# One planned order for all engines, turns of x on TensorE, and an early load of half of u, in a kernel of convolution and attention

## Chip, cores and metric

One core of a Trainium2 chip. The metric is the device time of one execution in microseconds, the median of several; a profile of one execution gives the views quoted here. The runs below were in the fast state, but for one of replan (591.53 us) and three of the kernel before beside the experiments (699.75, 693.45 and 691.0 us); ratios use fast runs alone. They are the mean time of one kernel's fast runs over the mean of the kernel before in the same rounds on the same chip, so they are not quite the ratio of the medians quoted beside them.

## The reference

Two independent halves share the input length of 2048. The left half of the output is a long convolution whose kernel K is generated from six parameter arrays, the right half is attention over eight keys at stride two.

```python
def conv(u, A, B, C, log_dt, Dskip):            # u: 1 x 2048 x 1024, A, B, C complex 1024 x 128
    dt = exp(log_dt)[:, None]
    P = exp((dt * A)[:, :, None] * arange(2048))
    K = einsum("dn,dnl,dn->dl", C, P, dt * B).real
    y = irfft(rfft(u_padded) * rfft(K_padded))[:2048]
    return y + u * Dskip
def attention(x, wqkv, wo):                     # x: 1 x 2048 x 1024, 32 heads of 32
    q, k, v = (x @ wqkv) ...                    # each query sees keys at offsets 0, 2, ..., 14 back
    return softmax(q . k / sqrt(32)) @ v  ... @ wo
return concatenate([conv(...), attention(...)], axis=-1)      # bf16
```

## The kernel before

It has two stages. In stage 1, QKV and the generation of K are written in one hand-made interleaving. In stage 2 two generators, convolution and attention, are advanced in turn by step counts.

```python
# stage 1: x comes by sixteen DMA transposes; V is 2048 matmuls of 32 output rows
def load_x(self, par):
    for kt in range(8):
        nc.sync.dma_start_transpose(out=self.xT[:, kt, par*1024:(par+1)*1024], in_=self.xv[par][:, kt*128:(kt+1)*128])
# ... V, in v():
for kt in range(8):
    for h in range(4):
        nc.tensor.matmul(ps[32*h:32*h+32, ...], lhsT=self.xT[:, kt, t0:t0+32], rhs=self.wv[:, kt, :, h, :], ..., tile_position=(0, 32*h))

# stage 2, convolution: an FFT in steps; what step 1 makes of u and K goes out to HBM and comes back
def step1(self, hf, name, src):
    ...
    nc.tensor.matmul(pz[:, i, :], lhsT=self.l1[:, mt, :], rhs=src[:, ..., :], ...)   # 512 columns
    self.bal.copy(zs[...], pz[:], 1024)
    nc.sync.dma_start(out=Z[:, n2:n2+4, :], in_=zs[64*b:64*b+64])
def middle(self, hf):
    # load(p): zu, zk from HBM, issued by GpSimd; forward(p-1); back(p-2)
    for x in range(2):
        V.tensor_tensor(out=pr[:, x], in0=F[1][:], in1=kf[:, x:x+1, :].to_broadcast(...), op=ALU.mult)  # F[1] in PSUM
    ...
# stage 2, attention: one S and one O bank
for ct in range(8):
    S = self.pp.tile([128, 512], F32, name="S")
    for b in range(-1, NB):                      # 9 key blocks x 4 heads: 36 matmuls of 32 rows, 8 to 40 columns
        for h in range(4):
            nc.tensor.matmul(S[hs, o:o+n], lhsT=ks[hs, ct, kb:kb+32], rhs=qs[hs, ct, qa:qa+n], ..., tile_position=(32*h, 32*h))
    ...                                          # Exp (ACT), mask (DVE), two matmuls with ones, 36 for the values, Ln and Exp (ACT), product (DVE)
    yield
...
drive(conv(), 64 + 36 + 16, at.gen(), 80)        # advances the two generators by counts
```

The softmax here doesn't subtract the row's maximum and nothing guards it: scores larger than these inputs give would overflow.

## Time and profile before

| | before |
|---|---|
| time, median (range) | 691.88 us (686.53 to 692.02), 3 runs; with the runs beside the changed kernel 690.08, 4 runs |
| profiled span | 688.6 us |
| busy: PE, DVE, ACT, POOL | 485, 376, 369, 105 us |
| DMA | 116.19 MB |
| mean granted clock of TensorE | 0.846 |

The prediction below reads the page of this profile. Two windows split the span at the end of kernel generation and at the first work on K; the columns are busy us of PE, its weight loads, DVE, ACT and POOL with instruction counts, the granted clock, DMA share and GB/s.

```profile
0.00:242.70 242.70, 185.96 (x3706) 104.37 (x3707) 183.36 (x314) 186.51 (x297) 29.36 (x35) 0.95 0.40 100
...
271.00:688.60 417.60, 276.76 (x5646) 125.65 (x5645) 192.44 (x281) 176.14 (x301) 76.03 (x128) 0.77 0.80 210
```

The late window is where time lies idle: 418 us for 277 us of PE work at a clock of 0.77, with DMA at 0.80.

### The profile page before, as it was taken

How to read it: one execution, taken by the hardware profiler on the slowest of the kernel's cores; microseconds unless marked ns; L12 is line 12 of the kernel's file. 1: busy time of each engine (PE TensorE's matmuls, PEld its weight loads, DVE VectorE, ACT ScalarE, POOL GpSimd, SP SyncE). 2: the span in 40 equal slices, each digit the busy share in tenths (PEclk: the TensorE clock that was granted, in tenths of full speed). 3: DMA queues.
4: the chain of work that ended last, by engine and by line, in shares of the span. 5: the costliest groups of instructions: out<-in, count | busy, mean ns of one | idle time of the engine just before them, and what ended most of it. 6: DMA issues, size and time to landing. Idle time of an engine off the chain costs nothing.

```text
span 688.6 us, 23065 instructions
## 1 busy us (share of the span) xinstructions
PE 484.9 (70%) x10268; PEld 247.5 (36%) x10268; DVE 376.1 (55%) x595; ACT 369.0 (54%) x608; POOL 105.4 (15%) x163
## 2 busy tenths in 40 slices
PE   0284989899999785303775962569788885779866
PEld 0031546556556455102343431224332341223432
DVE  4758878768777802221544431245855862576442
ACT  3585798698798623102554432334646752656441
POOL 5400111010110000000010020000545644350000
PEclk9997999999999898655885955687997997699979
DMA  9980322132231164999585699375997899894685
GB/s 145 258 165 16 93 79 92 59 102 72 79 103 66 54 223 136 255 181 253 136 272 177 199 224 178 91 231 145 328 270 199 243 218 253 220 264 99 185 223 161
DMA packets 103891, 116.19 MB, mean 169 GB/s; under 512 B 46992, under 2 KB 84112, under 8 KB 102128
## 3 DMA queue, kind: packets, MB, share of 16 engines
q1 hardware_dynamic: 95376, 88.63, 49.3%
q0 software_dynamic: 8416, 26.10, 13.9%
q8 instruction: 80, 1.31, 0.8%
q14 instruction: 19, 0.16, 0.1%
HBM read 58.59 MB, written 50.33 MB: 158 GB/s over the span
## 4 chain that ended last, share of the span: by engine, by line
PE 35%; DVE 15%; DMA 15%; ACT 14%; issue 10%; SPq 3%; POOL 0%; ACTq 0%; DVEq 0%
PE cp L579 6%; PE ps L383 6%; DMA Zv<-vs 4%; PE psv L399 4%; DMA big<-Zv 4%; PE cp L627 3%; DVE OR L195 3%; PE O L566 3%; PE S L550 2%; PE pk L239 2%; PE cp L653 2%; DVE OL L224 2%; PE cp L669 2%; DVE OL L223 2%; DMA Kd<-K 2%
## 5 line engine op out<-in xcount | busy, mean ns | idle before, releaser
L383 PE MATMUL ps<-xT,w 128*128 128x512 bf16 x512 | 129.7, 403 | 53.7 <-DMA xT<-in_B_x_dram 32.8
L659 DVE TENSOR_TENSOR pr<-cp,kf 128x1024 bf16<-128x1024 f32 x64 | 75.7, 1219 | 42.7 <-ACT kf L499 33.5
L383 PEld LDWEIGHTS <-w 128*128 128x128 bf16 x512 | 49.1, 102 | 119.1 <-issue 61.9
L550 PE MATMUL S<-qs,ks 32*32 32x40 bf16 (+2 forms) x2304 | 38.9, 185 | 60.3 <-ACT pe L553 20.9
L579 PE MATMUL cp<-wosb,oT 128*128 128x512 bf16 x256 | 62.4, 397 | 4.7 <-ACT zs L499 2.8
L570 ACT ACTIVATE ln<-O 128x256 f32<-128x256 f32 x64 | 24.6, 384 | 73.2 <-PE O L566 66.3
L643 POOL DMA_DIRECT2D zk<-Zk x64 | 38.2, 600 | 164.3 <-PE S L550 82.9
L399 PE MATMUL psv<-wv,xT 128*32 128x256 bf16 x2048 | 62.2, 273 | 0.0
L550 PEld LDWEIGHTS <-ks 32*32 32x32 bf16 x2304 | 27.5, 96 | 93.7 <-issue 72.9
L643 POOL DMA_DIRECT2D zu<-Zu x64 | 38.1, 600 | 138.9 <-PE S L550 117.3
L572 DVE TENSOR_TENSOR oT<-O,ln 128x256 bf16<-128x256 f32 x64 | 27.0, 422 | 54.4 <-ACT ln L571 54.4
L627 PE MATMUL cp<-big,l 128*128 128x512 bf16 x128 | 43.2, 450 | 18.2 <-DMA big<-in_A_u_dram 12.9
L399 PEld LDWEIGHTS <-xT 128*32 128x32 bf16 x2048 | 52.5, 97 | 7.2 <-issue 6.4
L499 ACT CAST vs<-cp 128x1024 bf16<-128x1024 f32 x32 | 32.4, 1012 | 39.8 <-DMA Zv<-vs 26.3
L502 DVE CAST zs<-cp 128x1024 bf16<-128x1024 f32 x36 | 43.0, 1218 | 17.5 <-PE cp L627 17.4
L553 ACT ACTIVATE pe<-S 128x320 bf16<-128x320 f32 x64 | 27.7, 433 | 43.3 <-PE S L550 42.3
L554 DVE TENSOR_TENSOR pm<-pe,mk 128x320 bf16<-128x320 bf16 x64 | 20.3, 320 | 50.8 <-ACT pe L553 32.4
L669 PE MATMUL cp<-pr,m 64*128 64x512 bf16 x256 | 41.2, 423 | 7.7 <-ACT vs L499 5.5
L499 ACT CAST zs<-cp 128x1024 bf16<-128x1024 f32 x28 | 28.0, 1009 | 34.2 <-PE cp L627 22.1
L182 DVE TENSOR_SCALAR PA<-PH 128x1024 int32<-128x1024 int32 (+1 forms) x36 | 27.9, 775 | 27.2 <-ACT TL L186 19.4
L579 PEld LDWEIGHTS <-oT 128*128 128x128 bf16 x256 | 25.2, 102 | 37.2 <-issue 11.8
L653 PE MATMUL cp<-zu,m 128*64 128x512 bf16 x128 | 24.0, 437 | 20.0 <-ACT vs L499 13.2
(105 smaller groups left out, 750.2 us busy)
## 6 DMA issues: line engine op xcount, KB each, us to landing
Zu<-zs SPq DMA_DIRECT2D x32, 256.0 KB, 5.1
Zk<-zs SPq DMA_DIRECT2D x32, 256.0 KB, 5.5
zu<-Zu POOLq DMA_DIRECT2D x64, 128.0 KB, 6.3
zk<-Zk POOLq DMA_DIRECT2D x64, 128.0 KB, 6.1
Zv<-vs SPq DMA_DIRECT2D x64, 128.0 KB, 3.9
big<-Zv SPq DMA_DIRECT2D x16, 512.0 KB, 7.6
w<-in_B_wqkv_dram POOLq DMA_DIRECT2D x16, 256.0 KB, 4.9
QT<-sg SPq DMA_DIRECT2D x16, 256.0 KB, 2.1
```

The lines of the kernel that those rows point to most:

```text
L182: V.tensor_scalar(out=PA[:, 0:n, :], in0=PH[:, 0:n, :], scalar1=16384.0, scalar2=None, op0=ALU.add)
L383: nc.tensor.matmul(ps[:, h, :], lhsT=self.w[ct][:, kt, t, :], rhs=self.xT[:, kt, t0:t0 + 512], start=(kt == 0), stop=(kt == 7))
L399: nc.tensor.matmul(ps[32 * h:32 * h + 32, b * 256:b * 256 + 256].rearrange("p (c d) -> p c d", d=32), lhsT=self.xT[:, kt, t0:t0 + 32], rhs ...
L499: self.nc.scalar.copy(out=out, in_=in_)
L502: self.nc.vector.tensor_copy(out=out, in_=in_)
L550: nc.tensor.matmul(S[hs, o:o + n], lhsT=ks[hs, ct, kb:kb + 32], rhs=qs[hs, ct, qa:qa + n], start=True, stop=True, tile_position=(32 * h, 3 ...
L579: nc.tensor.matmul(po[:, h, :], lhsT=oT[:, ct, tt * 128:(tt + 1) * 128], rhs=self.wo[:, ct, h * 512:(h + 1) * 512], start=(ct == 0), stop= ...
L627: nc.tensor.matmul(pz[:, i, :], lhsT=self.l1[:, mt, :], rhs=src[:, rq * 4 + rp * 2 + i, :], start=True, stop=True)
L643: nc.gpsimd.dma_start(out=t[64 * ri:64 * ri + 64], in_=self.Z[n][hf][4 * p + ri:4 * p + 4:2].rearrange("ab n d -> n ab d"))
L653: nc.tensor.matmul(f[64 * ab:64 * ab + 64, ri, :], lhsT=w[:, ab, 64 * ri:64 * ri + 64], rhs=z[:, ab, :], start=True, stop=True, tile_posit ...
L659: V.tensor_tensor(out=pr[:, x], in0=F[1][:], in1=kf[:, x:x + 1, :].to_broadcast([128, 2, 512]), op=ALU.mult)
L669: nc.tensor.matmul(v[:, ab, :], lhsT=w[rs, t, :], rhs=pr[rs, x, y, :], start=(i == 0), stop=(i == 3), tile_position=(64 * ab, 0), skip_gro ...
```

## The change

The intent is to fill that window. Everything becomes one list of 1813 tasks with dependencies and rings of buffers, and one fixed order for all engines, worked out ahead and stored in the kernel. Within it, x and the parameters are loaded in rows and turned by TensorE; V uses full-width matmuls; what step 1 makes of u and K stays on chip; and half of u is rewritten and loaded into the space that the sine phases leave, while QKV still runs. The core of the diff (cut; the order table and nearly all else left out):

```diff
+ORDER = (
+    "XAAJABEAAABRAUgPaQEhABgOUAA5AFkBgQEcAGQBUQ9YD2QASAFxAdAA5ABsABEC3ACxASkA+QEdAmUPMABBACUCMAJ8AaEPLQI4..."   # cut: 1813 codes
+)
 ...
-    def load_x(self, par):
-        for kt in range(8):
-            self.tc.nc.sync.dma_start_transpose(out=self.xT[:, kt, ...], in_=self.xv[par][:, kt * 128:(kt + 1) * 128])
+    def turn(self, pool, idn, load, put, eng, strided, prio):
+        def mm(e):
+            st["ps"] = ps = self.ps.tile([128, 2, 8, 128], BF, name="ps")
+            for i in range(2):
+                for kt in range(8):
+                    nc.tensor.transpose(ps[:, i, kt, :], st["xn"][:, i, kt * 128:(kt + 1) * 128], idn[:])
 ...
-                for b in range(2):
-                    n2 = 16 * (2 * mt + b) + rq * 4
-                    nc.sync.dma_start(out=Z[:, n2:n2 + 4, :], in_=zs[64 * b:64 * b + 64])
+                def evac(e, pi=pi, w=w):
+                    copy(nc, e, z["t"][:, :, 16 * pi:16 * pi + 16], w["pz"][:].rearrange("x p (g k) -> x k (p g)", g=4))
 ...
+        def load_u(hf, after):
+            src = {}; slot = P(None, 0, ..., [opened if hf else phases, after], take=("big", "b2") if hf else "bu", prio=2.4 + 3 * hf)
 ...
-    drive(conv(), 64 + 36 + 16, at.gen(), 80)
+        seq = plan.order()
+        for t in seq:
+            st["ring"] = t.ring
+            ...
+            t.fn(t.pick)
```

## The prediction

> **What bounds the kernel now.** I read the engine sums first, then the 40 slices, then busy time by stage, the waits, and a stretch of the timeline.
>
> ```profile
> PE 484.9 (70%) x10268; PEld 247.5 (36%) x10268; DVE 376.1 (55%) x595; ACT 369.0 (54%) x608; POOL 105.4 (15%) x163
> ...
> PE   0284989899999785303775962569788885779866
> ...
> DVE  4758878768777802221544431245855862576442
> ...
> PEclk9997999999999898655885955687997997699979
> DMA  9980322132231164999585699375997899894685
> ...
> DMA packets 103891, 116.19 MB, mean 169 GB/s; under 512 B 46992, under 2 KB 84112, under 8 KB 102128
> ```
>
> No engine is full over the span. There are two regimes in it. In the first third (QKV, kernel generation) PE and DVE, and ACT with them, are mostly at 7 to 9 tenths and DMA at 1 to 3. Then comes a hole, and after it everything is at 3 to 7 tenths while DMA is at 7 to 9. Busy time by stage (columns: PE, weight loads, DVE, ACT, POOL, granted clock, DMA share, GB/s):
>
> ```profile
> 62.00:145.00 83.00, 73.76 (x1472) 41.94 (x1471) 68.47 (x119) 68.32 (x123) 5.42 (x6) 0.93 0.24 77
> ...
> 258.00:345.00 87.00, 36.40 (x1176) 22.78 (x1166) 26.05 (x61) 20.77 (x41) 0.00 (x0) 0.69 0.80 193
> 345.00:487.00 142.00, 95.07 (x2402) 47.45 (x2401) 58.05 (x91) 56.12 (x112) 7.80 (x14) 0.71 0.71 190
> 487.00:640.00 153.00, 121.18 (x1857) 47.91 (x1857) 89.97 (x103) 85.61 (x123) 68.22 (x115) 0.87 0.87 232
> ```
>
> The 229 us from 258 to 487 are the soft part: DVE does 84 us of work, ACT 77, PE 131, the last at a clock of 0.7. The waits say why (engine, line, what it waited for: total us, times, longest):
>
> ```profile
> POOL zu L643 <- PE S L550: 117.3, 2, 117.1
> ...
> ACT ln L570 <- PE O L566: 66.3, 50, 7.7
> ...
> DVE oT L572 <- ACT ln L571: 54.4, 41, 6.4
> ...
> PE ps L383 <- DMA xT<-in_B_x_dram: 32.8, 8, 27.0
> ...
> DVE K L299 <- PE pk L239: 28.0, 1, 28.0
> ```
>
> Attention with one S and one O bank goes round PE, ACT, DVE once per tile with little beside it; the spread of K goes through HBM; x arrives by DMA transposes until about 45 us. A stretch of the timeline shows one more:
>
> ```profile
> 412.79 0.39 PE L550 MATMUL S<-qs,ks 32*32 32x40 bf16 x26
> ...
> 418.57 0.18 PE L550 MATMUL S<-qs,ks 32*32 32x32 bf16 x1 [5.40 <-issue]
> ```
>
> PE stops in the middle of a score tile for 5.4 us with nothing to wait for. Such "issue" steps are 9.8% of the chain that ended last (0.098 x 689 = 67 us). My reading, not shown by the view, is that PE's instructions are late: the page has an instruction queue of 80 packets, 1.31 MB, which shares the DMA engines.
>
> **What the Trainium skill says.** (1) "VectorE: DVE Perf Modes", the perf-mode tier table: a tensor_tensor runs two elements a cycle in bf16 from SBUF and one with any PSUM operand. The trace agrees: the product from PSUM (line 659, 1024 elements) takes 1219 ns, the bf16 outer product from SBUF (line 215, 1024 elements) 686. (2) The same page, the three transpose paths: a 128x128 bf16 block takes 390 ns on TensorE and 1309 by DMA. Single transposes aren't in this trace; it shows the sixteen DMA transposes of x being issued over 24 us. (3) "TensorE: Matmul & The Clock Gate", what's actually happening: the array runs at half clock until it has been busy for a window of about 3.4 us, and falls back after an idle one. Agrees: clock 1.00 where PE was 99% busy (145 to 195 us), 0.69 where it was 42% busy. (4) "DMA: Bandwidth & Descriptors", specifications: transfers want 512 B or more for full rate. No view here tests it alone; 46,992 of 103,891 packets are smaller.
>
> **The change part by part.** It rewrites nearly everything into 1813 tasks in one fixed order, so I count work per engine with durations from the rows of before.
>
> PE, warm. Eight 512-column matmuls take 1.83 us (chain rows): Q and K 64 x 1.83 = 117; V, now 256 full-width matmuls instead of 2048 narrow ones, 32 x 1.83 = 59 (before 32 x 1.76: no gain). New: 11 turns of 16 transposes, estimated at 1 us each from 2048 columns at the matmul rate, 11. Kernel products 2048 small matmuls, about 32 with their gaps. Attention 64 x (0.28 + 0.48, start to start near 644 us) = 49. Projection 16 x 3.47 = 56. First FFT step 65,536 columns at 0.215 us per 512, 28. Middle forward: sixteen 256-column matmuls on four tiles instead of four 512-column ones on two, the same 0.46 us, 64 times, 29. Back 32 x 0.9 = 29, last 16 x 0.9 = 14, shift 3. Sum 427.
>
> ACT. Sines 77 (before 80; the trivial phase row is gone), amplitudes 40, Q and K evictions 32, kernel evictions 7, parameters 12, attention 28 + 25 + 27 = 79, table loads about 17. In the order table, 135 of the 221 movable copies carry ACT and 86 DVE: 135 x 1.01 = 136. Sum 400.
>
> DVE. Kernel generation by its rows 164, parameters 26, nine turns 13, six V copies 7, K spread 16, attention 47, other copies 71 x 1.22 = 86, and the middle products 64 x 0.69 = 44 in place of 75.7, because u's spectrum is copied to bf16 first. That copy is 32 new ones on ACT or DVE, so the pair of engines gains nothing from it: 32 us saved for some 36 added. Sum 403.
>
> So ACT + DVE rise from 745 to 803; PE's sum falls from 485 only by being warm. The gain is in packing. What leaves is DMA: Zu and Zk (8.4 MB each, written and read back, 33.5 MB) stay in SBUF, K goes SBUF to SBUF, attention's q and k loads become long runs, and 76 us of POOL issue work (128 loads of Z, 600 ns each, that wait behind PE) go. What comes is the rewriting of u, 4.2 MB in 32,768 pieces of 128 B, placed where DMA was at 0.25. Adding all transfers up I get 85 MB in place of 116.
>
> Phase A, until the kernel is generated. By the order, everything on DVE up to the last kernel product comes first: 164 + 26 + 13 + 7 = 210 us. ACT has 176 there; PE 32 V tasks, 49 halves of Q and K tiles, turns and kernel products, 59 + 90 + 11 + 32 = 192. So DVE bounds it, if only just. It ran at 78 to 82% in this stage before; with phases triple buffered, two ER buffers and the order made for it I take 93%, 226 us, and 7 us before its first useful work (before: 7.05). End at about 233. Before, DVE finished the same work near 242, and the first K copy came at 271 because the kernel matmuls sat late in PE's queue. Here seven Q and K tiles are held back instead, interleaved with step one of u, so PE has something to do while K is spread.
>
> Phase B, the rest. PE 427 - 192 = 235, ACT 400 - 176 = 224, DVE 403 - 210 = 193. PE leads by little. Three engines at this load, in fixed queues, over three large PSUM tiles and the S and O banks (which scores and values may now trade for a large one): I take 89% for PE, a little under what 200 to 250 us showed (45.5 of 50), giving 264. With 3 us for the last store: 233 + 264 + 3 = 500.
>
> **The rivals.** *DMA bounds phase B.* Attention loads 13, V of the FFT 8.4 out and 8.4 in, outputs 8.4, FFT matrices 6.3, second half of K and u 4.2, wo 2.1: 51 MB. At the 232 GB/s of 487 to 640 us that is 220 us, hidden; at the 190 of 345 to 487, 268 us, just as long as PE. Then the round trip of the FFT's V (one step of 20.12 us in the chain) and the like are exposed: 535. *Late instructions stay.* PE still has some 19,000 instructions, and attention's small ones are unchanged; against it, DMA carries a quarter less. If half of the 67 us remain unhidden: 533. *The fixed order slips.* In-order queues pass one late transfer to all engines, and each stop over 3.4 us cools PE; at 80% in phase B, 294: 530; with phase A at 85% as well, 254 and 294: 551. *Better than I think:* both phases at 97%, 223 + 242 + 3 = 468. *It is hidden anyway:* phase A can hardly shrink, DVE fills it; that is in my sum, and it is why I don't predict 450.
>
> **Range and chances.** 500 us. Low 468: both phases almost without gaps. High 546: one rival in full and part of another. To be at 678, 2% below now, phase B would have to run at 53%, as now, which needs DMA to be no lighter than it was. Faster by over 2%: 0.97; within 2%: 0.02; slower: 0.01.
>
> **What would show it.** First QKV matmul before 12 us, and x no longer a releaser of PE. DVE at 9 tenths up to about 230 us. Line sums: products at 0.65 to 0.7 us, DVE about 400, ACT about 400, PE 420 to 460. Granted clock above 0.92 from 250 us on. DMA about 85 MB. Attention's waits (66 and 54 us) down to a third. I am wrong if DMA stays at 9 tenths over phase B, if the issue steps are still near 10% of the chain, or if DVE falls below 85% in phase A.

## The result, and the profile after

556.64 us, median of 4 runs (551.0 to 557.85), against 690.08 us of the kernel before in the same rounds: ratio 0.8055, 95% interval 0.7986 to 0.8124. It is faster, as predicted, but the time lies 57 us above the predicted 500 and 11 us above the range. The profile is of the fastest of the four runs (551.0; the others took 555.57 to 557.85), so what is read from it below explains some 51 of the 57 us.

From the page of the changed kernel: engine sums, then the busy tenths of 40 slices, the granted clock, DMA.

```profile
PE 462.5 (84%) x9548; PEld 262.1 (48%) x9548; DVE 378.2 (69%) x677; ACT 381.3 (69%) x613; POOL 34.4 (6%) x56
...
PE   2869999698499879699786789998969888798976
...
DVE  4897999999998799343395786686655767542240
...
PEclk9979999899599979899796899998988999799988
DMA  8732259246622658373895766557747576583431
...
DMA packets 114636, 86.65 MB, mean 158 GB/s; under 512 B 60960, under 2 KB 102304, under 8 KB 113264
```

The hole in PE's row has gone and DMA is no longer at 9 tenths in the late part. The windows of the changed kernel, split at the end of the DVE work on K and just after the last kernel matmul:

```profile
0.00:222.00 222.00, 181.55 (x2581) 95.75 (x2584) 198.53 (x355) 179.90 (x285) 16.99 (x24) 0.92 0.54 133
...
231.00:549.20 318.20, 274.40 (x6675) 162.36 (x6672) 178.24 (x320) 198.84 (x324) 17.43 (x32) 0.93 0.60 178
```

The last kernel matmul ends at 230.5 us, against a predicted 233. The early phase was right. The late phase takes 318.7 us instead of 267, and in it PE is busy 274 us, not 235. The waits of the changed kernel (who, for what: total us, times, longest):

```profile
DVE oT L718 <- ACT ln L713: 22.8, 23, 4.3
ACT ln L712 <- PE O L707: 22.4, 20, 3.8
PE pk L377 <- issue: 19.4, 9, 2.9
...
PE cp L682 <- issue: 8.8, 4, 3.0
...
ACT ln L712 <- PE cp L707: 7.6, 9, 2.2
```

Attention's own waits fell from 66.3 and 54.4 us to 30.0 (22.4 and 7.6, as some tiles now lie in the large banks) and 22.8: to less than half, where a third was predicted. What is left at the head of PE's list are stops put down to "issue": PE waited for nothing that the profile shows, in the kernel matmuls (line 377) and in the scores (line 682). One of them in the timeline (start, duration, instructions):

```profile
439.09 0.38 PE L682 MATMUL cp<-qs,ks 32*32 32x8 bf16 x24
441.49 0.25 PE L682 MATMUL cp<-qs,ks 32*32 32x40 bf16 x12 [2.03 <-issue]
```

PE stops after 24 of 36 score matmuls for 2.03 us. In the trace's DMA records a packet of 16 KB of the instruction queue runs from 438.90 to 440.24 us; PE goes on 1.25 us after it has landed. All traces together show that this is no accident. In the eighteen of them PE has 297 stops over 0.8 us that are put down to issue, and 296 of these ended 1.1 to 1.8 us after such a packet had landed (all 20 of the changed kernel, all 13 of the kernel before). Of the 397 stops over 0.8 us that are put down to anything else, 21 did. So these stops are waits for instructions, which the prediction had called its own reading. A packet holds 256 instructions of 64 B: 1.21 MB in 74 packets for 19,096 PE instructions, and dup_small below has 4608 more and 18 packets more.

For the experiments I worked out from each trace's PE records how long the array was occupied after the last kernel matmul, from the start of each matmul to the start of the next or its own end, whichever is first. This is not an answer of the profile:

```
                last kernel    late      PE        idle   instruction packets
                matmul at      phase     occupied         in the late phase
after           230.5          318.8     274.7     44.0   53
```

Of the 274.7 us, 38.0 lie where the granted clock was one half, so about 19 would go at full clock; 255.7 remain. And in the late phase PE changes its tile shape (full array, 64 rows and columns, 32 by 32, and so on) 274 times. Where the shape stays, a 512-column matmul starts 215 ns after the one before; where it changes, 309 to 312 ns. So a change costs some 95 ns at full clock, 26 us in the phase by estimate.

### The profile page after: what moved, and what is told of

Same layout as the page of the kernel before. It is cut to its first block, busy times and chain, and to the rows that moved or that the text cites. A ratio compares the mean times of both kernels' runs of the same rounds, so it can differ in the third digit from the quotient of the medians.

```text
span 549.2 us, 21477 instructions
## 1 busy us (share of the span) xinstructions
PE 462.5 (84%) x9548; PEld 262.1 (48%) x9548; DVE 378.2 (69%) x677; ACT 381.3 (69%) x613; POOL 34.4 (6%) x56
## 2 busy tenths in 40 slices
DMA packets 114636, 86.65 MB, mean 158 GB/s; under 512 B 60960, under 2 KB 102304, under 8 KB 113264
## 3 DMA queue, kind: packets, MB, share of 16 engines
q8 instruction: 74, 1.21, 0.9%
## 4 chain that ended last, share of the span: by engine, by line
issue 45%; PE 24%; DVE 11%; ACT 7%; DMA 5%; SPq 5%; POOL 3%; POOLq 0%; ACTq 0%; DVEq 0%
PE ps L615 5%; PE ps L585 4%; PE cp L750 4%; SPq L624 4%; PE pk L377 3%; POOL m L835 2%; ACT TL L285 2%; DMA wv<-in_B_wqkv_dram 2%; DVE PH L276 2%; PE cp L867 1%; PE cp L911 1%; DVE OR L309 1%; DVE OL L341 1%; DMA Vt<-sg 1%; DVE PA L280 1%
## 5 line engine op out<-in xcount | busy, mean ns | idle before, releaser
L615 PE MATMUL ps<-wv,xT 128*128 128x512 bf16 x256 | 64.7, 408 | 5.5 <-DMA wv<-in_B_wqkv_dram 4.4
L465 ACT CAST sg<-ps 128x1024 bf16<-128x1024 f32 x42 | 41.7, 1005 | 16.7 <-PE ps L585 7.3
L615 PEld LDWEIGHTS <-xT 128*128 128x128 bf16 x256 | 26.3, 104 | 38.6 <-issue 10.5
L859 DVE TENSOR_TENSOR pr<-uf,kf 128x1024 bf16<-128x1024 bf16 x64 | 41.2, 686 | 4.7 <-ACT uf L465 3.7
L812 PE MATMUL cp<-l,big 128*128 128x256 bf16 x256 | 39.4, 298 | 6.0 <-ACT zu L465 2.2
L835 POOL DMA_DIRECT2D m<-c_m x32 | 17.4, 545 | 418.9 <-PE cp L867 228.2
L377 PE MATMUL pk<-OR,OL 128*32 128x21 bf16 x2048 | 22.4, 185 | 24.9 <-issue 19.4
L812 PEld LDWEIGHTS <-big 128*128 128x128 bf16 x256 | 33.8, 174 | 11.9 <-issue 8.0
L465 ACT CAST vs<-cp 128x1024 bf16<-128x1024 f32 x28 | 28.3, 1013 | 15.5 <-PE cp L867 15.3
L377 PEld LDWEIGHTS <-OL 128*32 128x32 bf16 x2048 | 20.7, 115 | 29.0 <-issue 28.8
L712 ACT ACTIVATE ln<-O 128x256 f32<-128x256 f32 x48 | 18.5, 386 | 22.7 <-PE O L707 22.4
L718 DVE TENSOR_TENSOR oT<-O,ln 128x256 bf16<-128x256 f32 x48 | 20.2, 421 | 19.9 <-ACT ln L713 15.3
L845 PEld LDWEIGHTS <-m 64*64 64x64 bf16 x1024 | 26.1, 111 | 13.8 <-issue 10.0
L276 DVE SCALAR_TENSOR_TENSOR PH<-p_xs,p_phs 128x256 int32<-128x256 f32 x84 | 30.1, 419 | 0.9 <-ACT TL L285 0.9
L682 PE MATMUL S<-qs,ks 32*32 32x40 bf16 (+1 forms) x1872 | 23.6, 178 | 7.5 <-issue 4.7
```

The lines of the kernel that those rows point to most:

```text
L276: V.scalar_tensor_tensor(out=PH[:, j, :], in0=xc, scalar=float(RS[k + j] + 128), in1=self.phs[h][:, cs], op0=ALU.mult, op1=ALU.add)
L377: nc.tensor.matmul(pkv[32 * g:32 * g + 32, q, :], lhsT=OL[:, ri, dh, :, dl], rhs=OR[:, ri, h * DH + dh, :, dl], start=(ri == 0), stop=(ri ...
L465: nc.scalar.copy(out=out, in_=in_)
L615: nc.tensor.matmul(st["ps"][:, b, :], lhsT=self.xT[:, kt, t0:t0 + 128], rhs=self.wv[:, kt, :], start=(kt == 0), stop=(kt == 7))
L682: nc.tensor.matmul(S[hs, o:o + n], lhsT=st["ks"][hs, ct, kb:kb + 32], rhs=st["qs"][hs, ct, qa:qa + n], start=True, stop=True, tile_positio ...
L812: nc.tensor.matmul(w["pz"][:, i, :], lhsT=src["t"][:, :, 4 * pi + i], rhs=self.l1[:, lk], start=True, stop=True, skip_group_check=True)
```

## The experiments

Five batches; each gives its ratio to the kernel before on its own chip. For the comparison with the changed kernel I take the difference from 0.8055, times the median of before in that batch (688, 688, 689, 684, 685 us). The interval of 0.8055 is 4.7 us to either side and that of an experiment some 3 to 5, so differences under 6 us are not resolved.

The theories at the start: **P**, PE's own time paces the late phase; **L**, the fixed order and the latency of waits do; **F**, instructions come late in runs of small matmuls.

### back_half: half of the matmuls of the FFT's back step dropped

```diff
-for i, (x, y, k) in enumerate(((0, 0, 0), (0, 1, 1), (1, 0, 1), (1, 1, 2))):
+for i, (x, y, k) in enumerate(((0, 0, 0), (0, 1, 1))):
```

> Half of the matmuls of the FFT's way back left out (result wrong on purpose): PE loses 128 matmuls of 124 ns warm, 16 us of its occupancy, all in the second phase; nothing else changes. Theory P (PE paces the second phase; my sum for it was too small): 14 to 20 us less than the changed kernel's 556.6, ratio to before about 0.78. Theory L (the fixed order and the waits round PE, ACT and DVE pace it, PE has slack): less than 5 us.

543.24 us, ratio 0.7903 [0.7857, 0.7948]: 10.5 us less, for 16 us of array time (128 matmuls of 124 ns). The output still passes the comparison, though half of a sum is missing, so the comparison is not sharp on the convolution. PE paces the phase, but only some 0.65 of its time shows.

### dup_big: 192 large matmuls added

```diff
-for i, (x, y, k) in enumerate(((0, 0, 0), ...)):
+for i, (x, y, k) in enumerate(3 * ((0, 0, 0),) + ((0, 0, 0), ...)):
```

> Six matmuls more in each of the 32 ways back (the first pair three times more, result unchanged): 192 x 124 ns = 24 us of PE occupancy in the second phase, only 384 PE instructions. Theory P: 22 to 28 us more than 556.6, ratio about 0.84. Theory L: under 10 us more.

567.19 us, 0.8273 [0.8212, 0.8333]: 15 us more for a planned 24 us of array time and 384 instructions. The same 0.6 as in back_half.

### dup_small: each score matmul issued twice

```diff
-        for b in range(-1, NB):
+        for b in 2 * list(range(-1, NB)):
```

> Every score matmul twice (result unchanged): 2304 x 11 ns = 25 us of PE occupancy, as in the run with 192 large ones, but 4608 PE instructions, 18 instruction packets of 16 KB more. Theory P alone: 22 to 28 us more, as there. Theory F (PE runs dry at packet borders inside small matmuls, some 1.2 to 2 us each, and cools): 20 us or more on top of that, 45 to 70 us in all, with issue waits before the score matmuls up from 13.5 to over 30 us. Theory L: under 10 us.

601.57 us, 0.8783 [0.8719, 0.8848]: 50 us more, for about the same planned array time, 25 us, but 4608 instructions. PE's waits in this kernel:

```profile
PE S L682 <- issue: 22.8, 19, 2.2
PE pk L377 <- issue: 19.3, 9, 3.0
PE O L707 <- issue: 7.2, 5, 2.7
PE cp L682 <- issue: 6.4, 4, 2.6
```

and in dup_big, where the scores are untouched:

```profile
PE pk L377 <- issue: 20.1, 9, 2.7
PE S L682 <- issue: 7.8, 6, 2.2
```

The added small instructions are paid for in stops by issue (37.9 us within scores and values, 13.3 in dup_big) and in the clock: 67.3 us of the late phase are occupied at half clock, 40.8 in dup_big. The late phases are 369.7 and 339.0 us, with 71 and 55 packets: 1.9 us for each packet more. (These are single traces; in the medians it is 34 us, 2.1 each.) The array time is not more: with the half-clock time counted at full clock, PE is occupied 14 us more than in the changed kernel, in dup_big 18. The 51 us of dup_small's late phase are thus some 14 of array time, 15 of half clock and 22 of idle time. This is the strongest sign for theory F.

### act_light: ACT work taken away

Wrong result: the Exp that makes the reciprocal is dropped.

```diff
-        self.tc.nc.scalar.activation(out=ln[:], in_=ln[:], func=ACT.Exp, scale=-1.0)
```

> The Exp of the reciprocal left out (result wrong on purpose): ACT loses 64 x 0.42 = 27 us in the second phase and each attention tile's round becomes 0.4 us shorter. Theory P: under 6 us less than 556.6. Theory L: 12 us or more less.

549.44 us, 0.8008 [0.7967, 0.8049]: 3 us less, not resolved. 27 us of ACT work in the middle of attention's chain are worth next to nothing, so ACT's time does not pace the phase. I took this as the end of theory L, which was too wide a conclusion: it speaks of ACT, not of the order.

### u_linear: u rewritten in long rows

Wrong result: the rewriting of u copies rows of 8 KB in place of 128 B pieces.

```diff
-in_=self.uv[:, :, c0 + 64 * c2:c0 + 64 * c2 + 64]
+in_=self.uv[16 * hf + 4 * g + 2 * c2:16 * hf + 4 * g + 2 * c2 + 2].rearrange(...)      # contiguous
```

> Wrong result on purpose: u is copied into its rewritten place in rows of 8 KB instead of pieces of 128 B, the same bytes to the same places in the queue, so that some 32,000 packets go. If those small packets hold up the 16 KB instruction packets in the kernel generation (theory: the fetch is slow because the rewriting of u shares the transfer engines), the idle time of PE put down to issue ahead of the kernel matmuls (19.4 us) falls below 10 us and the time by 3 to 8 us (552 to 547, for a kernel after of some 555). If the fetch is slow by itself (my theory), that idle time stays at 15 to 22 us and the time within 3 us.

559.02 us, 0.8121 [0.8061, 0.8181]: 4.5 us more, not resolved. The page counts 32,256 packets fewer, and the stops ahead of the kernel matmuls are 20.7 us. The small pieces do not hold up the instructions.

### x_dma: x by DMA transposes again

The turns of x are undone, with 64 DMA transposes of 256 rows on SP's queue; the parameters are still turned on TensorE.

```diff
-            q.dma_start(out=xn[:], in_=self.xv[par][r * 256:(r + 1) * 256, :].rearrange(...))      # then 16 transposes on PE
+            for kt in range(8):
+                self.tc.nc.sync.dma_start_transpose(out=self.xT[:, kt, b * 256:(b + 1) * 256], in_=...)
```

> One part of the change undone: x comes by 64 DMA transposes of 256 rows again, issued on one queue; the parameters are still turned on TensorE. Theory that the turns on TensorE carry much of the gain: PE has no x until 25 to 45 us, QKV starts late, and as PE has only 40 us of slack up to the end of kernel generation, the last kernel matmul moves from 230 to 240 or later: 10 to 20 us slower. Rival: kernel generation on DVE sets that end alone and QKV work only fills, DVE is even relieved of some turns: within 4 us of after.

605.16 us, 0.8781 [0.8719, 0.8843]: 50 us more, far over the 10 to 20 that I expected. The last kernel matmul moves by just as much, from 230.5 to 280.5 us, and one line of DVE's waits tells how:

```profile
DVE sg L467 <- DMA Vt<-sg: 38.3, 1, 38.3
```

DVE's fixed queue holds an eviction of V that needs a staging buffer, whose store sits on SP's queue behind the transposes. DVE, the busiest engine of this phase, stands still once for 38.3 us. So the 50 us are not the worth of the turns alone: the order was made for x by TensorE, and 64 issues (13% of the chain that ended last, on SP's sequencer) are more than the sixteen of the kernel before. The fixed order passes one late transfer on to the busiest engine.

### mix_pk: small and large matmuls woven one by one

Right result. Each run of 16 kernel-matmul groups is woven with four halves of Q, K or V tiles, one large matmul after every 16 small.

```diff
+WOVEN = (((pk, pk, pk, pk), (half,), 32, 8), ...)      # 16 units
+            small, large = run(unit[0]), run(unit[1])   # issue in even shares
```

> Same arithmetic, right result. The four runs of 16 kernel-matmul groups (512 small matmuls, 1024 instructions each) are woven one by one with four halves of Q, K or V tiles each: one large matmul after every 16 small ones, so a 16 KB packet of instructions lasts some 3 us instead of 2 or less. Theory F (instruction packets come late in runs of small matmuls): idle time by issue ahead of the kernel matmuls falls from 19.4 us to under 8 us; as DVE sets the end of this stage, the total falls by only 0 to 5 us. Rival (the gaps have another cause, such as PSUM banks or weight loads of small tiles): 15 to 22 us stay.

574.21 us, 0.8335 [0.8277, 0.8392]: 19 us more, where I expected 0 to 5 us less. The group of kernel matmuls (busy us, mean ns, idle before and what ended it), first in the changed kernel, then in mix_pk:

```profile
L377 PE MATMUL pk<-OR,OL 128*32 128x21 bf16 x2048 | 22.4, 185 | 24.9 <-issue 19.4 <-DVE OR L309 3.5 <-ACT kraw L465 1.8
```

```profile
L393 PE MATMUL pk<-OR,OL 128*32 128x21 bf16 x2048 | 41.2, 188 | 13.4 <-DVE OR L325 10.5 <-ACT kraw L482 2.9
```

The stops by issue are gone altogether, which theory F had said; yet the busy time nearly doubles, and the last kernel matmul comes at 251.5 us. The timeline of mix_pk shows the new cost:

```profile
98.58 0.51 PE L633 MATMUL ps<-wv,xT 128*128 128x512 bf16 x1
99.01 0.32 PE L393 MATMUL pk<-OR,OL 128*32 128x21 bf16 x16
99.27 0.61 PE L633 MATMUL ps<-wv,xT 128*128 128x512 bf16 x1
```

Each large matmul and the 16 small ones beside it take 0.7 to 0.8 us at this place. From 95 to 252 us there are 262 changes of tile shape, 14 in the changed kernel over the same time, and the start-to-start time at them is 320 ns after a large matmul instead of 216.

### mix_att: scores and values woven with their neighbours

Right result; 102 of the 128 score and value tasks woven in the same way.

> Same arithmetic, right result. 102 of the 128 score and value tasks of attention are woven with their neighbours in PE's order (halves of the projection, FFT matmuls), instruction by instruction, nothing else moves. Theory F and PE paces: issue gaps within scores and values (about 15 us with those over 0.8 us) fall below 7 us, half-clock time falls, total 6 to 12 us faster than after (0.978 to 0.99 of it). Rival (order and latency): scores and values end later by a large task, ACT and DVE wait for them: 3 to 10 us slower.

825.88 us, 1.2012 [1.1941, 1.2083]: slower than the kernel before. Both theories missed it. A window of the late phase of this kernel, columns as above:

```profile
400.00:700.00 300.00, 285.75 (x3426) 129.59 (x3425) 98.50 (x145) 96.88 (x157) 10.78 (x20) 0.63 0.33 92
```

PE is busy 95% of the time by the profile and is granted a clock of 0.63. From 271 us on the trace has 1477 changes of shape. Worked out as for the table above, PE is occupied 546.5 us in the late phase, 384.8 of them at half clock. At full clock that would be 354 us, 98 more than in the changed kernel, or 82 ns for each of 1203 changes more; the half clock adds 173 us more, and idle time is as before (44.6 us). That makes up the 272 us. Why the clock falls is not shown. It is not long stops: the longest in this window is 1.51 us. Nor is it the changes of shape alone: mix_pk's clock was 0.96, 0.81 and 0.93 from 95 to 140, to 175 and to 252 us, where the changed kernel with 14 changes has 0.92, 0.81 and 0.93. Weaving is the wrong way to space small instructions out.

### alt_pk: the order of mix_pk without the weaving

Four kernel-matmul groups and one half tile in turn, as whole tasks; only the order table differs.

> Right result. The order of mix_pk without its weaving: four kernel-matmul groups (256 instructions) and one half of a Q, K or V tile in turn, whole tasks. Theory F with the request spacing read from the traces (two 16 KB packets are never requested less than 3.43 us apart, and four groups take 1.1 us of array time, a half tile 1.73): stalls stay but shrink, issue idle ahead of the kernel matmuls 8 to 14 us instead of 19.4. Theory that mix_pk lost by draining the array at each change of tile shape (some 95 ns each, 256 of them, and the half clock after them): without weaving its 17 to 20 us vanish, last kernel matmul at 229 to 235, time within 4 us of after. Rival (delaying QKV halves costs mix_pk its time): stays 10 us or more above after.

555.83 us, 0.8091 [0.8041, 0.8141]: 2.5 us more, not resolved. The loss of mix_pk came from the weaving, with its 262 changes of shape (alt_pk has 32 over the same time), not from the later QKV halves. And:

```profile
L377 PE MATMUL pk<-OR,OL 128*32 128x21 bf16 x2048 | 23.1, 185 | 21.5 <-DVE OR L309 11.0 <-ACT kraw L465 6.0 <-issue 4.3
```

Of 19.4 us of stops 4.3 are left (I expected 8 to 14), but the idle time before this group hardly moves: PE now waits for DVE and ACT instead, and the last kernel matmul comes at 235.8 us, no earlier. The stops of PE in the early phase cost nothing by themselves.

### u_late: half of u loaded after QKV, as it would be without the early load

```diff
-            [opened if hf else phases, after], take=("big", "b2") if hf else "bu"
+            [opened, after], take=("big", "b2")
-            if hf == 0 and name == "u":
-                self.plan.then(freed, right)                 # (the order table moves with it)
```

> One part of the change undone: the first half of u is loaded only after QKV, into the other large buffer, and its first FFT step comes after that of K instead of between the last Q and K tiles; the rest of the order is kept. If the early load carries its part of the gain, PE has less to do while K is spread and the load stands on the path: 8 to 16 us slower than after (about 565). Rival, hidden anyway (phase B has some 44 us of idle PE time to take it up): within 4 us.

553.24 us, 0.8022 [0.7948, 0.8095]: 2 us less, not resolved. The last kernel matmul is at 232.0, the late phase is 321.2 us. The third part of the change, by itself, is hidden: the late phase has room for it.

### replan and replan_blind: other orders of the same tasks

Right results, only the order table differs (and which of ACT or DVE makes some copies). Both come from a local search on a model of the queues with PE durations from the trace; the model of replan_blind has no instruction packets, changes of shape or half clock.

> Right result, same 1813 tasks, another order (and another choice of ACT or DVE for some copies, of the PSUM ring for some tiles), found by local search on a model of the queues with PE durations measured in the trace of after: 0.27 us per kernel-matmul group, 0.43 per FFT step, 0.1 per change of tile shape, 3.47 us least between instruction packets, half clock for 3.4 us after a stop of 1.8. The model puts after at 526 (measured span 549) and this at 478. Theory O (the fixed order itself holds phase B, by waits spread thin over all engines): 495 to 525 us, PE idle falls by 25 us or more. Theory P alone (PE's own time paces, order is near its best): 545 to 560.

> The same search as replan, but its model knows nothing of instruction packets, changes of tile shape and half clock. Its order judged by the full model: 486, 8 us above replan. If instruction fetch and cooling are a main cause of the lost time, it is 8 us or more slower than replan, with more issue idle within scores, values and kernel matmuls; if they are minor, within 4 us of it.

replan: 584.76 us (one of its four runs slow, left out of the ratio), 0.8486 [0.8416, 0.8556]. replan_blind: 566.59 us, 0.8241 [0.8181, 0.8301]. Both are slower than the changed kernel, by 30 and 13 us, and the one that should have been better is worse. The model was wrong, not only the theories: it had taken the transfer times of the kernel's own planner. In the trace, SP needs 0.5 to 0.6 us to issue most transfers (the eight stores of a V task take some 4.1, planned 2.0; two stores of the FFT 1.2, planned 0.15). With issue as measured and a fitted landing time the same model puts the four orders in the measured sequence (541, 550, 564, 573 for spans of 549, 557, 562, 580). In replan PE waits 15.3 us for the loads of the FFT's V, where the changed kernel has no such wait. The packed orders had left no slack for the transfers.

### sp_relief: half of the FFT's transfers on another queue

```diff
-nc.sync.dma_start(out=self.Zv[hf][4 * p + ri:...], ...)
+(nc.gpsimd if ri else nc.sync).dma_start(out=self.Zv[hf][4 * p + ri:...], ...)          # and the loads of V likewise, by b
```

> Right result, order of after. Half of the stores and of the loads of the FFT's V (48 of 96 transfers, some 28 us of issue time) are issued on POOL's queue instead of SP's. If SP's in-order queue is one of the limits of phase B (the mended model gives 11 us for a quarter of all its issue times): 3 to 8 us faster than after (0.99 of it). Rival (the queue of SP is idle enough): within 2 us, or slower because POOL's loads of the FFT matrices then wait behind the stores.

554.98 us, 0.809 [0.8019, 0.8161]: 2 us more, not resolved. In the order as it stands SP's queue is not what holds the late phase.

### replan_dma: the search with the measured transfers

> Right result, same tasks. The search of replan again, its model mended by what the traces of after, replan and replan_blind show of DMA: 0.5 to 0.65 us to issue each transfer on the queue of SP (a task of 8 stores 4.2 us, not 2.0), landing 2.5 us after the issue at the least, transfers one after the other at 400 KB/ms times 1000. So mended it puts after, alt_pk, replan_blind and replan at 541, 550, 564 and 573, where the spans were 549, 557, 562 and 580. It puts this order at 485, PE idle 52 us in place of 99. Theory O (the order, with issue and landing of transfers in it, holds the late phase): 495 to 525. Rival (the model is still short of what matters, PE's own work and its clock pace): 545 or more.

543.03 us, 0.7943 [0.7896, 0.7989]: 8 us less than the changed kernel, in neither of the expected ranges. The last kernel matmul comes at 221.5 us, 9 us earlier, and the late phase is 318.0 us, as before. A better order helps the early phase; the late phase does not yield to it. (Its model had instruction packets too, but counted them cheap.) Stops by issue within scores and values are 19.6 us, up from 17.0.

### few_small: fewer small instructions, same columns

Wrong result: two key blocks share one matmul of 80 columns.

```diff
-        for b in range(-1, NB):
+        for b in (-1, 0, 2, 4, 6):
-            qa, n = (0, 8) if b < 0 else (32 * b, 40 if b < NB - 1 else 32)
+            qa, n = (0, 8) if b < 0 else (32 * b, 80) if b < 6 else (184, 72)               # scores; values likewise, 72 or 64
```

> Wrong result on purpose: attention's 32-row score and value matmuls are issued two key blocks at a time (80 columns instead of twice 40), so the same columns come out with 4096 instructions fewer, 16 packets of 256; order and everything else as in after. Theory F (small instructions cost more than their array time, as dup_small said: some 1.9 us per packet on top of the array time): array time falls by 10 to 15 us, worth 6 to 10 at the 0.65 that back_half showed, and 16 packets fewer give 15 to 30 more: 20 to 40 us faster than after (0.93 to 0.965 of it). Theory P (array time alone): 6 to 10 us faster.

530.93 us, 0.7757 [0.7724, 0.779]: 20 us less, at the lower edge of what F said and twice the upper end of P. The waits of this kernel have one line left for stops by issue within scores and values:

```profile
PE S L682 <- issue: 0.4, 1, 0.4
```

17.0 us became 0.4, with 37 packets instead of 53 in the late phase. The late phase is 295.3 us, 23.5 shorter: 19.7 of it PE occupation and 3.8 idle time. At half clock 21.3 us are occupied instead of 38.0, which is 8.3 us of the 19.7; the other 11.4 are array time. At the 0.65 of back_half those are worth 7.4 us, so some 13 of the 20 us belong to the instruction stream and the clock, 0.8 us for each of 16 packets. The idle time falls little because short waits (under 0.8 us) grow from 14.0 to 18.4 us: the next limit takes over.

### replan_fetch: an order that spaces small instructions out

The search of replan_dma with a dearer instruction packet. Right result.

> Right result, same tasks, meant as the better version. The search of replan_dma with a dearer model of instruction packets: a packet can be used 4.7 us (not 2.3) after PE came within 290 instructions of its end, because stops of 2 to 4 us within values and scores (25 us in the late phase) came back in replan_dma, which the old model had put at almost nothing. The new model puts after at 555, replan_dma at 520 and this at 491. Spans were 549 and 540. Theory F: 510 to 532, with issue idle within scores, values and the FFT's matmuls down to half. Rival: 535 to 550, if the search only bends the model.

531.70 us, 0.7773 [0.7733, 0.7813]: 19 us, or 3.5%, faster than the changed kernel (0.7773/0.8055 = 0.965), and faster than both; that is just inside the range of theory F. From its page:

```profile
PE 449.1 (85%) x9489; PEld 258.4 (49%) x9548; DVE 372.7 (70%) x674; ACT 378.1 (71%) x614; POOL 33.2 (6%) x56
...
PEclk9979999998999999989998969999999999999999
```

Its stops by issue at the kernel matmuls, the values and the scores:

```profile
PE cp L707 <- issue: 5.9, 5, 3.5
...
PE O L707 <- issue: 3.0, 2, 1.8
PE cp L682 <- issue: 1.7, 2, 1.0
...
PE pk L377 <- issue: 0.6, 1, 0.6
```

The last kernel matmul is at 221.8 us, as in replan_dma, and the late phase 307.6, 10 us shorter than there and 11 shorter than in the changed kernel. All stops of PE by issue are 17.4 us instead of 37.4, but 18.8 of these 20 us lay ahead of the kernel matmuls, in the early phase, where alt_pk showed them to cost nothing. Within scores and values they went from 17.0 to 10.6, and 3.7 us came up in the FFT: not down to half. At half clock 21.3 us are occupied in place of 38.0, which is worth 8 of the 11 us. Idle time is 44.2 us, unchanged, and so is the part of it in stops over 0.8 us (26 us for 25). So the gain in the late phase is in the clock. That the clock rose because PE waited less for instructions is argued, not shown.

The late phases side by side, worked out from the traces as above:

```
                last kernel    late      PE        idle   instruction packets
                matmul at      phase     occupied         in the late phase
after           230.5          318.8     274.7     44.0   53
back_half       231.0          312.2     261.4     50.9   52
dup_big         231.5          339.0     294.4     44.6   55
dup_small       228.6          369.7     303.2     66.5   71
act_light       231.3          318.7     272.0     46.8   53
u_late          232.0          321.2     271.9     49.3   53
alt_pk          235.8          321.1     270.3     50.8   53
few_small       231.0          295.3     255.0     40.2   37
replan_dma      221.5          318.0     272.9     45.1   53
replan_fetch    221.8          307.6     263.4     44.2   52
```

## Why the prediction was right and wrong

**Direction and early phase: right.** DVE at 9 tenths almost to the end, the last kernel matmul at 230.5 us for 233 predicted. The close hit has some luck in it: DVE was busy 198.5 us up to 222 us, 89%, not 210 us at 93% of 226, so less work and looser packing offset each other. The first QKV matmul started at 13.4 us (27.0 before), not before 12. That PE's stops do not set this end is shown by alt_pk, where they went and the end did not move forward; that DVE does is read from its share alone, and replan_dma reached this end 9 us earlier by order. The weight of x by TensorE is bounded by x_dma, though the 50 us there are mostly one wait of 38.3 us that the fixed order made.

**Sizes of work: right.** Products at 686 ns, DVE 378 and ACT 381 for some 400 each, PE 462 just above 420 to 460, DMA 86.65 MB for 85. Attention's waits fell less than predicted, as said above. The rival *DMA bounds phase B* did not come: DMA is at 0.60 there.

**Late phase: wrong.** The step that failed is "Phase B, the rest", its PE term of 235 us at 89%, making 264 and 3. Measured: 274.7 us occupied and 44.0 idle. The 51.8 us over it split like this:

- Some 20 us of array time that the sum did not have: 255.7 us at full clock instead of 235. By kind the trace gives attention 58.8 us (predicted 49), the middle forward step 34.1 (29), the first FFT step 32.0 (28) and the back step 31.1 (29); projection, last step, shift and the late QKV halves are within 2 us. The sum counted each kind by the rate of an undisturbed run and had no term for changing the tile shape; 274 changes at 95 ns are 26 us by estimate, and all but 13 of them follow a matmul of attention, the forward or back step, or the projection. That a change costs time is measured within the traces, and mix_pk and alt_pk, the same order with and without weaving, fit it. That it is just these 20 us is argued, and the first FFT step, with 7 changes, needs another reason. The trace of the kernel before could have told: its late phase has 314 changes, and its attention takes 54 us at full clock, not 49.
- 19 us of half clock. The prediction named the mechanism, stops that cool PE, but used warm durations throughout, and it counted only stops over 3.4 us as cooling; here no stop of the late phase is over 3.0 us and 38.0 us run at half clock. Its sign "clock above 0.92 from 250 us on" came true, at 0.93, and such a mean already holds this loss.
- 12 us of idle time more than the 29 that 89% leaves and the 3 for the last store.

The last two are in good part the rival *Late instructions stay*, which I had given half of 67 us and left out of the central sum: of the idle time 17.0 us are stops for instructions. Not all of the half clock follows them: 13.7 of the 44.4 us that the late phase was granted at half clock come after short waits for ACT and DVE. The rival's mechanism is what the runs support: dup_small (50 us for 4608 small instructions, where 24 us of large ones cost 15), few_small (20 us back for 4096 fewer), and 296 of 297 stops that end just after an instruction packet has landed. replan_fetch fits (half-clock time from 38.0 to 21.3 us by order alone). The chain that I built its size on was a poor gauge: after the change it puts 45% on issue, because it passes over waits of POOL, so my test "near 10% of the chain" could not decide anything. The waits of PE itself can. In the kernel before they were, ahead of scores, values and kernel matmuls:

```profile
PE S L550 <- issue: 19.9, 7, 6.6
PE O L566 <- issue: 8.4, 3, 4.5
PE pk L239 <- issue: 5.7, 5, 1.9
```

That is 34.0 us, half of the 67 that the chain gave. After the change it is 37.4. The late instructions stayed in full.

The rival *The fixed order slips* is half right. It gave 530 for a late phase at 80%, and PE is at 86% there. The order does matter: five other orders of the same tasks lay between 532 and 585 us. But a shorter late phase came only from the search that counted an instruction packet as dear (4.7 us after PE came near its end); replan_dma, which knew the transfers and counted packets at 2.3 us, moved the early phase.

*Hidden anyway* was applied to the kernel generation only. The runs show it for the early load of u (u_late) and for PE's stops in the early phase (alt_pk).

**Still open.** Of the 44 us of idle time in the late phase, 25 are stops over 0.8 us, 14 shorter waits and 5 come after the last matmul, and no experiment here brought the sum below 40. Why a packet comes late is not settled either: over the eighteen traces two 16 KB packets are never requested less than 3.23 us apart (the 3.43 in the expectation of alt_pk is the changed kernel's trace alone), and at 58 of the 297 stops the packet was requested only after PE had run dry, but whether the fetch or the dispatch of 256 instructions sets that pace no run tells.

## What to carry to other kernels

Count instructions as well as array time: a run of small matmuls that uses up 256 PE instructions faster than packets came here (at least 3.23 us apart) can leave PE without instructions, and the stop can cost again through the clock. Space such runs out by whole tasks, not matmul by matmul, since a change of tile shape cost some 95 ns here. And judge a planned order by a model that has been checked against several measured orders: with planned instead of measured issue times, the search made the kernel 5% slower, and with measured ones and dearer packets 3.5% faster.

## What the Trainium skill lacked or had wrong

- "Runtime: NRT & Kernel Launch", section "Instruction fetch mechanics": the Trainium skill says that PE's instruction memory is refilled in blocks of 16 KB, 256 instructions, that crossing a block is mostly hidden, and that fetch is hidden because dispatch is slower. The block size agrees (74 packets for 19,096 PE instructions). That it is hidden does not hold in runs of small matmuls: single stops of 2 to 3 us, 37.4 us in all in the changed kernel, and 1.9 us for each packet added in dup_small. The least spacing of two requests, 3.23 us over eighteen traces, is not on the page.
- "TensorEngine Tiling (Array Packing)", section "Key Properties": the Trainium skill says that a change of tiling mode drains the array, without a figure. Here it is some 95 ns for each change at full clock (309 to 312 ns in place of 215 between starts), 26 us by estimate in the late phase of the changed kernel.
- "TensorE: Matmul & The Clock Gate", section "A second HAM failure mode: psum-queue depth-cycling": the Trainium skill tells of short idles between groups of matmuls that let the clock swing. A clock that stays low while PE is nearly always busy is not there: in mix_att, where small and large matmuls are woven, PE was busy 285.75 of 300 us by the profile, at a granted clock of 0.63. What in the weaving does it is open.
- I found on no page a time, measured on Trainium2, that SP's queue needs to issue one transfer ("DMA: Bandwidth & Descriptors" has only a cycle count for earlier generations, in a table on trn3): 0.5 to 0.6 us here for most, some 4.1 us for the eight of a V task. That the planner's shorter figures made replan slower is argued from a model that puts four orders in the measured sequence.
